# A decode block on one core: V in 64 KB runs and one transfer a head, head 0's keys in the repeated body, wq in 32 KB runs

## The chip, the cores and the metric

The kernel runs on one core of one Trainium2 chip. The metric is the device time of one execution in microseconds (us); lower is better. Inputs lie in HBM, TensorE (PE) multiplies 128x128 tiles out of SBUF into PSUM, VectorE (DVE) and ScalarE (ACT) work on PSUM and SBUF, and SyncE (SP) issues the transfers, which all run on the core's 16 DMA engines. A profile row "PE L566" is an instruction of TensorE recorded at line 566; "PEld" is its weight load.

## The reference

One token passes through a transformer block: layer norm, attention of 32 heads over a cache of 32768 keys and values each, output projection and residual, then a second layer norm and a dense layer with a mish activation.

```python
# B=1, D=512, H=32, Dh=128, Sk=32768, F=1376, all bfloat16
def _A_ref(x, k_cache, v_cache, wq, wo):
    q = (x @ wq).reshape(B, Sq, H, Dh).transpose(0, 2, 1, 3)
    scores = jnp.einsum("bhqd,bhkd->bhqk", q, k_cache) * (Dh ** -0.5)
    p = softmax(scores)
    o = jnp.einsum("bhqk,bhkd->bhqd", p, v_cache)
    return o.transpose(0, 2, 1, 3).reshape(B, Sq, H * Dh) @ wo
def _B_ref(x, w1, b1, w2):
    h = jnp.einsum("bsd,df->bsf", x, w1) + b1
    sp = log1p(exp(-abs(h))) + where(h > 0, h, 0)
    return jnp.einsum("bsf,fd->bsd", h * tanh(sp), w2)
h  = x + _A_ref(layernorm(x), k_cache, v_cache, wq, wo)
h2 = h + _B_ref(layernorm(h), w1, b1, w2)
```

The K and the V of one head are 8 MB each, so 512 MB are read from HBM for one token.

## The kernel before

**Slots.** SBUF holds a ring of six slots of 4 MB (32 KB in each of 128 partitions). Slots 0 and 1 take the two halves of a head's K, slots 2 and 3 those of its V, slot 4 wq and later the small weights of the end, slot 5 wo. Head 0's K is an exception: its halves go into slots 2 and 3 (`HOMES`), so that head 1's K can be fetched without waiting for anything, and head 0's V then waits for head 0's K.

**Transfers.** `order` is the list of all transfers, and SP issues them in that order (`start`, L439): wq, K of head 0, wo, then for each head h its two K halves and the two V halves of head h-1, at the end the rows of wo for the last head, the two V halves of head 31, w1 and w2. Ahead of each it waits until its slot is free (`freed_by`): a K or V half waits for the same half of the head before it. A half takes keys `half*16384` and on, and partition p holds 128 neighbouring keys of that half, one run of 32 KB in HBM. The first V half of head 31 (`SPLITV`) is issued in two pieces and the second (`LASTV`) in four (64, 32, 16 and 16 keys a partition), so that the work at the end can follow the data closely. wq is read as four runs of 8 KB in each partition (`(k p) n -> p k n`), with x laid out to match by a small matmul (L498).

**Work.** For each K half (`keys`, `k_group`) PE transposes 128 tiles (L566), eight to a group, DVE copies each group out of PSUM (L569), and PE forms the scores with the query as moving operand, one column for each tile (L544, three groups behind). The softmax needs the maximum over all 32768 scores (L610 to L623, with two small matmuls), one `exp` on ACT (L626) and a sum (L631). `pv` multiplies the V tiles with the probabilities (L595, 256 matmuls a head), and `oev` divides by the sum (L605).

**Order on the engines.** Head 0's keys and softmax are written out straight. Then `S.rounds(1, H, head, rest, mid)` makes a loop on PE and DVE: round i does `head(i)` (keys and maximum of head i) and `rest(i)` (the sum of head i-1, its `pv` in three parts with the steps `soft_a` and `soft_b` of head i between them, `oev`, and the `exp` of head i). In PE's loop the blocks lie in memory in the order top, head, mid, rest; `mid` (output projection of heads 0 to 30) runs once, in place of `head`, before the `rest` of the last round. The code of the second half of the block, `project_last` and on, follows the loop. `in_final` puts a wait into the loop body that holds only in the last round.

Of the kernel before, what the change touches and what calls it, by code (L numbers as in the profile page):

```python
# [21 lines left out]
class _Sched:  # L22
# [73 lines left out]
    def rounds(self, first, end, head, rest, mid):  # L96


        both = (head, rest)
        self.end = end  # L100
        if not self.emit:
            for n in range(first, end):
# [4 lines left out]
                self._play(tuple(LOOPED), n, (rest,), self.log["rest"])  # L107
            mid()
            self.log[PE][end] = {}
            self._play((PE,), end, (rest,), self.log["rest"])  # L110
            return
        if self.only == PE:
            self._pe_rounds(first, end, head, rest, mid)
            return
        if self.only == DVE:
# [3 lines left out]
            with self.nc.Fori(first, end, engines=OrderedEngineSet([e]), hint_back_edge=True,  # L119
                              head_slot={e: 0}) as i:  # L120
                self.counter = i
                self._play(tuple(LOOPED), first, both)
            self.counter, self.mute = None, True
            for n in range(first + 1, end):
                self._play(tuple(LOOPED), n, both)
            self.mute = False
        else:
            for n in range(first, end):
                self._play(tuple(LOOPED), n, both)
        mid()  # L130
        self._play((PE,), end, (rest,), self.log["rest"])

    def _pe_rounds(self, first, end, head, rest, mid):
# [3 lines left out]
        names = [f"rounds_{x}_{nc.next_id()}" for x in ("top", "head", "mid", "rest", "done")]  # L137
        top, n_head, n_mid, n_rest, done = names
# [4 lines left out]
        self.reg = regs[e]  # L143
        with nc.body(top, valid_engines=on):
            hint = t.mark_branch_hint_location()
            t.br_eq(regs[e], end, on_true=n_mid, on_false=n_head)
        with nc.body(n_head, valid_engines=on):
            self.loop_waited = {}
            self.counter = nc.snap(regs, min_val=first, max_val=end - 1)
            self._play(tuple(LOOPED), first, (head,))  # L150
            nc.br(n_rest, engines=on)
        self.counter = None
        with nc.body(n_mid, valid_engines=on):
            self.uncounted = True
            mid()
            self.uncounted = False
            nc.br(n_rest, engines=on)
        with nc.body(n_rest, valid_engines=on):
            self.loop_waited = {}
            self.counter = nc.snap(regs, min_val=first, max_val=end)  # L160
            self._play(tuple(LOOPED), first, (rest,), self.log["rest"])
# [4 lines left out]
        for n in range(first + 1, end):  # L166
            self._play(tuple(LOOPED), n, (head, rest))
# [5 lines left out]
    def in_final(self, eng, wait):  # L173
        if eng != PE or not self.emit or self.only != PE or self.counter is None:
            return
        with self.engines[PE].If_eq(self.reg, self.end):
            self.engines[PE].wait_ge(self._handle(wait[0]), wait[1])
# [80 lines left out]
def build_kernel(nc, A_x, A_k_cache, A_v_cache, A_wq, A_wo, B_w1, B_b1, B_w2, out):  # L258
    D = A_x.shape[-1]
    Dh = 128  # L260
# [65 lines left out]
    b1r = sb([FJ + 1, 128], BF16, "b1r")  # L326
    lnx = sb([128, 2, 2, 128], F32, "lnx")
# [21 lines left out]

    sem = nc.alloc_semaphore  # L350
    kinds = [PE, ACT, DVE, POOL, SP, "exp", "pmax", "gmax", "qc", "nb", "rcp", "oev", "A", "B", "C", "qkh", "pv", "fv", "ov"]
# [3 lines left out]
    s_x = sem("s_x")  # L355
    s_b1 = sem("s_b1")
# [14 lines left out]
    SPLITV = ("v", H - 1, 0)  # L371
    LASTV = ("v", H - 1, HALVES - 1)
    TAIL = [64, 32, 16, 16]
    piece_sems = [sem(f"piece{i}") for i in range(1, len(TAIL))]

    s_wl = sem("wl")
    s_early = sem("early")
# [5 lines left out]
    AFTER = {WQ: [], WO: [], WL: [WQ]}  # L383
    for half in range(HALVES):
        HOMES["k", 0, half] = HALVES + half
        AFTER["k", 0, half] = AFTER["k", 1, half] = []
        AFTER["v", 0, half] = [("k", 0, half)]

    def slot_of(what):
# [4 lines left out]
        return what[2] + (HALVES if what[0] == "v" else 0)  # L394
# [14 lines left out]
    def freed_by(what):  # L409
        if what[0] in ("w1", "w2"):  # L410
            return []
        if what == SPLITV:
            return [f"early{H - 2}"]
        if what in AFTER:
            return [free_name(x) for x in AFTER[what]]
# [10 lines left out]
    wol_v = w12[:, W2:W2 + D]  # L426

    events = {}

    def program(S):  # L430
# [10 lines left out]
        for what in order:  # L441
# [3 lines left out]
            if what[0] == "wq":  # L445
                start(wq_v, A_wq.rearrange("(k p) n -> p k n", k=KC), ready[slot])
# [13 lines left out]
            else:  # L460
                kind, h, half = what
                cache = A_k_cache if kind == "k" else A_v_cache
                rows = cache[0, h, half * 128 * TPS:(half + 1) * 128 * TPS, :].rearrange("(p r) d -> p (r d)", r=TPS)
                if what == SPLITV:
                    at = TPS // 2 * Dh
                    start(flat[:, 0:at], rows[:, 0:at], s_early)
                    S.wait(SP, [free_name(("v", H - 2, 0))])
                    start(flat[:, at:], rows[:, at:], ready[slot])
                elif what == LASTV:
                    at = 0  # L470
                    for n, s in zip(TAIL, [ready[slot]] + piece_sems):
                        start(flat[:, at * Dh:(at + n) * Dh], rows[:, at * Dh:(at + n) * Dh], s)
                        at += n
                    assert at == TPS
                else:
                    start(flat, rows, ready[slot])
# [5 lines left out]
        S.dma(ACT, lambda: a.dma_start(xr[:, :], A_x[0, 0, :].rearrange("(c m) -> c m", c=KC)).then_inc(s_x, 16))  # L482
        if S.emit and S.only == ACT:
# [16 lines left out]
        S.step(DVE, lambda: v.tensor_copy(lnx[:, 0, 0, 0:128:32], X_REG), name="lnh0", waits=["xT"])  # L500

        def layernorm(n):
# [12 lines left out]
            S.step(ACT, lambda: a.activation(rstd, lnv, ACTF.Exp, scale=-0.5), name=f"lnr{n}", waits=[f"lnln{n}"])  # L515
# [21 lines left out]
        def scores(h, col0, bg):  # L537
            last = col0 + GT == SCOLS
            for r in range(GT):
                names = [f"qkh{h}"] if last and r == GT - 1 else []  # L540
                waits = [f"ev{bg}"] if r == 0 else []
                if r == 0 and col0 == 0:
                    waits += [f"qc{h}"] + ([f"exp{h - 1}"] if h >= 1 else [])
# [32 lines left out]
        def pv(h, half, r0, r1):  # L576
            what = ("v", h, half)
            vt = tiles_of(what)
            for r in range(r0, r1):
                col = half * TPS + r  # L580
                waits = []
                if col == 0:
                    waits.append(f"exp{h}")
                if r == 0:
                    waits.append(ready_wait(what))
                elif half == HALVES - 1 and r in starts:
                    S.in_final(PE, (piece_sems[starts.index(r) - 1], 16))
                names = []
                if half == 0 and r == 0:
                    S.in_final(PE, (s_early, 16))  # L590
                if half == 0 and r == TPS // 2 - 1:
                    names = [f"early{h}"]
                if r == TPS - 1:
                    names = [free_name(what)] + ([f"pv{h}"] if half == HALVES - 1 else [])
                S.step(PE, lambda r=r, col=col: t_.matmul(o_ps[:, 0:1], vt[:, r, :], pbuf[:, col:col + 1],  # L595
                                                          start=(col == 0), stop=(col == SCOLS - 1)),
                       name=(names or None), waits=waits, kind="pv" if half == HALVES - 1 else ("ov" if r < TPS // 2 else "fv"))

        starts = [sum(TAIL[:i]) for i in range(len(TAIL))]

# [85 lines left out]
        S.rounds(1, H, head, rest, mid)  # L686
# [3 lines left out]
        S.step(DVE, lambda: v.tensor_tensor(lnx[:, 1, 0, 0:128:32], yps[:, 0:KC], lnx[:, 0, 0, 0:128:32], ALU.add), name="lnh1", waits=["y"])  # L690
# [75 lines left out]
```

## Time and profile before

| | |
|---|---|
| median of 3 runs | 1282.67 us (1282.5 to 1282.84) |
| profiled execution: its own time | 1282.67 us |
| profiled execution: span, first to last instruction | 1280.9 us |
| bytes read from HBM | 548.21 MB, 428 GB/s over the span |
| busy: PE, PE weight loads, DVE, ACT | 80%, 77%, 56%, 2% |
| chain that ended last, by engine | DMA 82%, PE 13%, DVE 2%, issue 2% |

The span leaves out 1.77 us that lie around the first and the last instruction. The rate is a mean over the span; the rows of the 40 slices tell how it runs in time. The chain follows the last instruction back, at each step to what released it: a share of a transfer in it is time in which the next work waited for that transfer or for the transfers queued ahead of it.

### The profile page before, as it was taken

The page shows a single profiled execution, that of the slowest core. Times are in us where ns is not written, and L with a number is a line of the kernel's source. Part 1 is how long each engine was busy: PE and PEld are TensorE (multiplying, and loading weights), DVE is VectorE, ACT ScalarE, POOL GpSimd, SP SyncE. Part 2 cuts the span into 40 slices and gives each one's busy share as a digit, 9 for nine tenths or more (in the row PEclk, how much of TensorE's full clock was granted, in tenths as well). Part 3 has the DMA queues.
Part 4 walks back from the last instruction along what each step waited for, and adds up shares of the span by engine and source line. Part 5 has one row for each costly group of instructions (what it writes and reads, how often), then busy time and mean ns, then how long its engine had stood idle before and what let it go on. Part 6 is the DMA issues. An engine that isn't in the chain of part 4 may idle for free.

```text
span 1280.9 us, 52609 instructions
## 1 busy us (share of the span) xinstructions
PE 1019.4 (80%) x25125; PEld 990.5 (77%) x25125; DVE 711.4 (56%) x1248; ACT 20.6 (2%) x70; POOL 1.8 (0%) x8
## 2 busy tenths in 40 slices
PE   3869977779877789877798777798777898777886
PEld 3768877779777788777788777797777787777885
DVE  2746664456654456644566544566544566444661
ACT  0000000000000000000000000000000000000000
POOL 0000000000000000000000000000000000000000
PEclk9878876778876788776788776788777788677885
DMA  9999999999999999999999999999999999999998
GB/s 404 428 423 435 432 429 434 432 431 433 430 434 432 430 435 431 431 433 430 434 432 430 433 433 429 433 432 432 432 430 435 431 430 433 433 431 433 430 418 343
DMA packets 21873, 548.47 MB, mean 428 GB/s; under 512 B 2304, under 2 KB 3808, under 8 KB 4576
## 3 DMA queue, kind: packets, MB, share of 16 engines
q1 hardware_dynamic: 21784, 548.22, 99.7%
q8 instruction: 13, 0.21, 0.1%
q14 instruction: 4, 0.03, 0.0%
q0 software_dynamic: 64, 0.00, 0.0%
q10 hardware_dynamic: 8, 0.00, 0.0%
HBM read 548.21 MB, written 0.00 MB: 428 GB/s over the span
## 4 chain that ended last, share of the span: by engine, by line
DMA 82%; PE 13%; DVE 2%; issue 2%; SPq 0%; ACT 0%; DVEq 0%
DMA ring<-in_A_v_cache_dram 81%; PE ops L595 9%; PE tps L566 2%; DVE ering L569 2%; DMA ring<-in_A_k_cache_dram 2%; PE sps L544 1%; SPq L439 0%; PE sps L701 0%; PE hlp L616 0%; PE hlp L621 0%; PE tps L717 0%; PE hlp L631 0%; PE hlp L508 0%; DVE pmax L610 0%; ACT lns L513 0%
## 5 line engine op out<-in xcount | busy, mean ns | idle before, releaser
L566 PE MATMUL tps<-identb,ring 128*128 128x128 bf16 x8192 | 667.2, 232 | 187.9 <-DMA ring<-in_A_k_cache_dram 185.0
L569 DVE COPY ering<-tps 128x1024 bf16<-128x1024 bf16 x1024 | 668.2, 692 | 236.9 <-PE tps L566 230.2
L566 PEld LDWEIGHTS tps<-identb,ring 128*128 128x128 bf16 x8192 | 521.1, 104 | 191.3 <-DMA ring<-in_A_k_cache_dram 187.5
L544 PE MATMUL sps<-qcur,ering 128*128 128x1 bf16 x8192 | 343.2, 164 | 7.7 <-DVE ering L569 6.7
L544 PEld LDWEIGHTS sps<-qcur,ering 128*128 128x128 bf16 x8192 | 308.8, 97 | 10.8 <-DVE ering L569 9.8
L595 PEld LDWEIGHTS ops<-pbuf,ring 128*128 128x128 bf16 x8192 | 223.8, 103 | 57.6 <-DMA ring<-in_A_v_cache_dram 35.9
L595 PE MATMUL ops<-pbuf,ring 128*128 128x1 bf16 x8192 | 232.0, 165 | 40.0 <-DMA ring<-in_A_v_cache_dram 35.1
L605 DVE TENSOR_TENSOR oT<-ops,rtotc 128x1 f32 x31 | 5.0, 161 | 142.2 <-PE ops L595 142.2
L618 DVE TENSOR_REDUCE gmax<-hlp 1x1 f32<-1x128 f32 x32 | 8.9, 278 | 65.6 <-PE hlp L616 65.6
L623 DVE TENSOR_SCALAR nbias<-hlp 128x1 f32<-128x1 f32 x32 | 5.1, 158 | 65.0 <-PE hlp L621 65.0
L626 ACT ACTIVATE pbuf<-sps,nbias 128x256 bf16<-128x256 f32 x32 | 15.2, 474 | 1231.4 <-PE ops L595 1184.9
L610 DVE TENSOR_REDUCE pmax<-sps 128x1 f32<-128x256 f32 x32 | 13.6, 425 | 15.4 <-PE sps L544 15.4
L621 PE MATMUL hlp<-gmax,onesmat 1*128 1x1 f32 x64 | 18.3, 353 | 0.4 <-DVE gmax L618 0.4
L616 PE MATMUL hlp<-ident,pmax 128*1 128x128 f32 x64 | 17.4, 369 | 0.5 <-DVE pmax L610 0.5
L631 PE MATMUL hlp<-esum,onesmat 128*128 128x1 f32 x64 | 12.3, 262 | 6.0 <-issue 5.9
L621 PEld LDWEIGHTS hlp<-gmax,onesmat 1*128 1x128 f32 x64 | 15.6, 300 | 1.1 <-DVE gmax L618 0.7
L631 PEld LDWEIGHTS hlp<-esum,onesmat 128*128 128x128 f32 x64 | 9.9, 195 | 8.3 <-issue 6.0
L523 PE MATMUL hlp<-xnT,ring 128*128 128x1 bf16 x128 | 3.6, 165 | 9.7 <-DMA ring<-in_A_wq_dram 9.7
L523 PEld LDWEIGHTS hlp<-xnT,ring 128*128 128x128 bf16 x128 | 3.5, 104 | 9.8 <-issue 9.8
L633 DVE RECIPROCAL rtotc<-hlp 128x1 f32<-128x1 f32 x32 | 5.1, 159 | 10.1 <-PE hlp L631 10.1
L605 DVE TENSOR_TENSOR oL<-ops,rtotc 128x1 bf16<-128x1 f32 x1 | 0.2, 163 | 12.0 <-PE ops L595 12.0
L527 DVE CAST qT<-hlp 128x32 bf16<-128x32 f32 x1 | 0.2, 191 | 11.9 <-PE hlp L523 11.9
(59 smaller groups left out, 41.4 us busy)
## 6 DMA issues: line engine op xcount, KB each, us to landing
ring<-in_A_k_cache_dram SPq DMA_DIRECT2D x64, 4096.0 KB, 26.8
ring<-in_A_v_cache_dram SPq DMA_DIRECT2D x62, 4096.0 KB, 31.3
ring<-in_A_v_cache_dram SPq DMA_DIRECT2D x3, 2048.0 KB, 11.3
ring<-in_A_wq_dram SPq DMA_DIRECT2D x1, 4096.0 KB, 12.4
ring<-in_A_wo_dram SPq DMA_DIRECT2D x1, 4096.0 KB, 41.6
ring<-in_B_w_dram SPq DMA_DIRECT2D x1, 1376.0 KB, 18.1
ring<-in_B_w_dram SPq DMA_DIRECT2D x2, 640.0 KB, 20.1
ring<-in_A_v_cache_dram SPq DMA_DIRECT2D x1, 1024.0 KB, 13.5
```

Of the source, the lines that this page charges most:

```text
L523: S.step(PE, lambda h=h, kc=kc: t_.matmul(Q_REG[:, h:h + 1], wq_v[:, kc, h * Dh:(h + 1) * Dh], xnT[:, 0, kc:kc + 1], start=(kc == 0), stop ...
L544: S.step(PE, lambda r=r: t_.matmul(S_ps[:, col0 + r:col0 + r + 1], ering[:, bg % NE, r, :], qcur[:, :], start=True, stop=True), name=(name ...
L566: S.step(PE, lambda r=r: t_.matmul(tb[:, r * 128:(r + 1) * 128], kt[:, gi * GT + r, :], identb[:, :], is_transpose=True, start=True, stop= ...
L569: S.step(DVE, lambda: v.tensor_copy(ering[:, bg % NE, :, :].rearrange("p r d -> p (r d)"), tb[:, :]), name=f"ev{bg}", waits=[f"trb{bg}"], ...
L595: S.step(PE, lambda r=r, col=col: t_.matmul(o_ps[:, 0:1], vt[:, r, :], pbuf[:, col:col + 1], start=(col == 0), stop=(col == SCOLS - 1)), n ...
L605: S.step(DVE, lambda: v.tensor_tensor(out_column(), o_ps[:, 0:1], rtotc[:, :], ALU.mult), name=f"oev{h}", waits=[f"pv{h}", f"rcp{h}"], kin ...
L610: S.step(DVE, lambda: v.tensor_reduce(pmax[:, :], S_ps[:, 0:SCOLS], AXX, ALU.max), name=f"pmax{h}", waits=[f"qkh{h}"], kind="pmax")
L616: S.step(PE, lambda: t_.matmul(A_REG, pmax[:, :], ident[:, :], start=True, stop=True), name=f"A{h}", waits=[f"pmax{h}", "ident", f"rcp{h - ...
L618: S.step(DVE, lambda: v.tensor_reduce(gmax[:, :], A_REG, AXX, ALU.max), name=f"gmax{h}", waits=[f"A{h}"], kind="gmax")
L621: S.step(PE, lambda: t_.matmul(B_REG, onesm[0:1, :], gmax[:, :], start=True, stop=True), name=f"B{h}", waits=[f"gmax{h}", "consts0"], kind ...
L626: S.step(ACT, lambda: a.activation(pbuf[:, :], S_ps[:, 0:SCOLS], ACTF.Exp, bias=nb[:, :], scale=SC, accum_out=esum[:, :]), name=f"exp{h}", ...
L631: S.step(PE, lambda: t_.matmul(C_REG, onesm[:, :], esum[:, :], start=True, stop=True), name=f"C{h}", waits=[f"exp{h}"], kind="C")
```

## The change

- V of heads 0 to 29 is one transfer of 8 MB into slots 2 and 3 together. Partition p holds keys 256p to 256p+255, one run of 64 KB in HBM. The V of head 30 is issued in two halves and that of head 31 in the six pieces that it had before, in the new layout (`PARTS`); each piece waits for the step of the head before that has read the same columns (`v_done`).
- K follows the same layout of keys, since scores and V must match: a half is a run of 32 KB out of each 64 KB of HBM.
- Head 0's K goes into slots 0 and 1 as every other, so head 1's K now waits for it, and head 0's V waits for nothing.
- The loop on PE starts with head 0: `head(0)` is its body in round 0, and a new block `turn` (the softmax of head 0) stands ahead of `top` and is entered from the end of `head` in round 0 alone. The straight code for head 0's keys goes. The blocks lie in the order turn, top, mid, head, rest. On the other engines head 0 is written out straight as before.
- wq is read as one run of 32 KB in each partition (`(p k) n -> p (k n)`), and x comes in a second time in the matching layout by a transfer of 8 bytes a partition on ACT's queue (`xc`). The old layout of x, by way of the matmul, is kept for the residual (`xres`).
- The waits of the last rounds (`in_round`) name their round; the body of `rest` has six of them, where it had four.

```diff
-    def _pe_rounds(self, first, end, head, rest, mid):
+    def _pe_rounds(self, end, head, turn, rest, mid):
...
-        nc.regs_mov(regs, first)
-        t.addr_align(256, offset=0, max_nops=0)
+        nc.regs_mov(regs, 0)
         nc.br(top, engines=on)
         self.reg = regs[e]
+        with nc.body(n_turn, valid_engines=on):
+            turn()
+            nc.regs_alu(regs, regs, 1, op=ALU.add)
+            t.addr_align(256, offset=0, max_nops=0)
+            nc.br(top, engines=on)
         with nc.body(top, valid_engines=on):
             hint = t.mark_branch_hint_location()
             t.br_eq(regs[e], end, on_true=n_mid, on_false=n_head)
...
+        with nc.body(n_head, valid_engines=on):
+            self.loop_waited = {}
+            self.counter = nc.snap(regs, min_val=0, max_val=end - 1)
+            self._play(tuple(LOOPED), 0, (head,))
+            t.br_lt(regs[e], 1, on_true=n_turn, on_false=n_rest)
...
+    V_EVENTS = (TPS // 2, TPS)
+    PARTS = {H - 2: [(0, TPS), (TPS, SCOLS)],
+             H - 1: [(0, TPS // 2), (TPS // 2, TPS), (TPS, 192), (192, 224), (224, 240), (240, SCOLS)]}
     order = [WQ] + halves("k", 0) + [WO]
     for h in range(1, H):
-        order += halves("k", h) + halves("v", h - 1)
-    order += [WL] + halves("v", H - 1) + W1P + W2P
+        order += halves("k", h) + [("v", h - 1)]
+    order += [WL, ("v", H - 1)] + W1P + W2P
...
     def freed_by(what):
-        if what[0] in ("w1", "w2"):
+        if what == WL:
+            return [free_name(WQ)]
+        if what[0] not in ("k", "v") or what[1] == 0 or (what[0] == "v" and what[1] in PARTS):
             return []
...
-        return [free_name((what[0], what[1] - 1, what[2]))]
+        return [free_name((what[0], what[1] - 1) + what[2:])]
     def tiles_of(what):
-        return ring[:, slot_of(what), :].rearrange("p (r d) -> p r d", d=Dh)
+        n = 1 if len(what) > 2 else HALVES
+        return ring[:, slot_of(what):slot_of(what) + n, :].rearrange("p s (r d) -> p (s r) d", d=Dh)
+    def keys_of(cache, h):
+        return cache[0, h, :, :].rearrange("(p r) d -> p r d", r=SCOLS)
...
-                start(wq_v, A_wq.rearrange("(k p) n -> p k n", k=KC), ready[slot])
+                start(flat, A_wq.rearrange("(p k) n -> p (k n)", k=KC), ready[slot])
...
-                rows = cache[0, h, half * 128 * TPS:(half + 1) * 128 * TPS, :].rearrange("(p r) d -> p (r d)", r=TPS)
...
+                if what[0] == "k":
+                    start(tiles_of(what), keys_of(A_k_cache, h)[:, what[2] * TPS:(what[2] + 1) * TPS, :], ready[slot])
+                    continue
+                for n, (r0, r1) in enumerate(PARTS.get(h, [(0, SCOLS)])):
+                    if h in PARTS:
+                        S.wait(SP, [v_done(h - 1, r1)])
+                    start(tiles_of(what)[:, r0:r1, :], keys_of(A_v_cache, h)[:, r0:r1, :],
+                          piece_sems[h][n - 1] if n else ready[slot])
...
+        S.dma(ACT, lambda: a.dma_start(xc[:, :], A_x[0, 0, :].rearrange("(p k) -> p k", k=KC)).then_inc(s_xc, 16))
...
-        S.step(DVE, lambda: v.tensor_copy(lnx[:, 0, 0, 0:128:32], X_REG), name="lnh0", waits=["xT"])
+        S.step(DVE, lambda: v.tensor_copy(lnx[:, 0, 0, 0:128:32], xc[:, :]), name="lnh0", waits=["lnz", (s_xc, 16)])
+        S.step(DVE, lambda: v.tensor_copy(xres[:, :], X_REG), name="xres", waits=["xT"])
...
-        keys(0, 0)
-        keys(0, 1)
-        flush(0)
-        soft_max(0)
-        soft_a(0)
-        soft_b(0)
-        soft_exp(0)
+        def turn():
+            soft_a(0)
+            soft_b(0)
+            soft_exp(0)
...
             soft_c(t)
-            pv(t, 0, 0, TPS // 2)
+            pv(t, 0, TPS // 2)
             S.unless_final(PE, "soft_a", lambda: soft_a(i))
-            pv(t, 0, TPS // 2, TPS)
+            pv(t, TPS // 2, TPS)
             S.unless_final(PE, "soft_b", lambda: soft_b(i))
-            pv(t, 1, 0, TPS)
+            pv(t, TPS, SCOLS)
             oev(t)
...
-        S.rounds(1, H, head, rest, mid)
+        S.rounds(H, head, turn, rest, mid)
```

More of the change, by code (lines that the diff above doesn't have):

```diff
@@ L94, in _play, with rounds @@
         self.round, self.looped = None, ()
-    def rounds(self, first, end, head, rest, mid):
-        both = (head, rest)
+    def rounds(self, end, head, turn, rest, mid):
         self.end = end
         if not self.emit:
-            for n in range(first, end):
+            for n in range(end):
                 for e in LOOPED:
@@ L110, in rounds @@
             self._play((PE,), end, (rest,), self.log["rest"])
+            del self.log[DVE][0]
             return
         if self.only == PE:
-            self._pe_rounds(first, end, head, rest, mid)
+            self._pe_rounds(end, head, turn, rest, mid)
             return
+        head(0)
+        turn()
         if self.only == DVE:
@@ L165, in _pe_rounds @@
         self.mute = True
-        for n in range(first + 1, end):
-            self._play(tuple(LOOPED), n, (head, rest))
+        for n in range(1, end):
+            self._play(tuple(LOOPED), n, (head, rest) if n > 1 else (head,))
         mid()
@@ L171, in _pe_rounds, with in_round @@
         nc.switch_bb(done)
-    def in_final(self, eng, wait):
+    def in_round(self, eng, n, wait):
         if eng != PE or not self.emit or self.only != PE or self.counter is None:
             return
-        with self.engines[PE].If_eq(self.reg, self.end):
+        with self.engines[PE].If_eq(self.reg, n):
             self.engines[PE].wait_ge(self._handle(wait[0]), wait[1])
@@ L348, in build_kernel @@
     OX_PS = T_f[2][:, 0:32]
+    V_EVENTS = (TPS // 2, TPS)
     sem = nc.alloc_semaphore
-    kinds = [PE, ACT, DVE, POOL, SP, "exp", "pmax", "gmax", "qc", "nb", "rcp", "oev", "A", "B", "C", "qkh", "pv", "fv", "ov"]
+    kinds = [PE, ACT, DVE, POOL, SP, "exp", "pmax", "gmax", "qc", "nb", "rcp", "oev", "A", "B", "C", "qkh", "pv"] + [f"pv{r}" for r in V_EVENTS]
     kinds += [f"{k}{i}" for k in ("ev", "tr") for i in range(2 * GPS)]
@@ L355, in build_kernel @@
     s_x = sem("s_x")
+    s_xc = sem("s_xc")
     s_b1 = sem("s_b1")
@@ L460, in program @@
             else:
-                kind, h, half = what
-                cache = A_k_cache if kind == "k" else A_v_cache
-                rows = cache[0, h, half * 128 * TPS:(half + 1) * 128 * TPS, :].rearrange("(p r) d -> p (r d)", r=TPS)
[L464 to L476, printed above, removed]
+                h = what[1]
+                if what[0] == "k":
[6 more added lines that the diff above has]
+                          piece_sems[h][n - 1] if n else ready[slot])
         S.dma(SP, lambda: sp.dma_start(out[0, 0, :].rearrange("(c m) -> c m", c=KC), outr[0:128:32, :]).then_inc(s_out, 16),
@@ L573, in k_group, with pv @@
             flush(KEEP)
-        def pv(h, half, r0, r1):
-            what = ("v", h, half)
+        def pv(h, r0, r1):
+            what = ("v", h)
             vt = tiles_of(what)
             for r in range(r0, r1):
-                col = half * TPS + r
                 waits = []
-                if col == 0:
-                    waits.append(f"exp{h}")
                 if r == 0:
[L585 to L599, printed above, removed]
+                    waits += [f"exp{h}", ready_wait(what)]
+                for n in PARTS:
+                    for i, (first, _) in enumerate(PARTS[n][1:]):
+                        if r == first:
+                            S.in_round(PE, n + 1, (piece_sems[n][i], 16))
+                names, kind = [], "pv"
+                if r + 1 in V_EVENTS:
+                    names, kind = [f"pv{h}_{r + 1}"], f"pv{r + 1}"
+                if r == SCOLS - 1:
+                    names, kind = [free_name(what), f"pv{h}"], "pv"
+                S.step(PE, lambda r=r: t_.matmul(o_ps[:, 0:1], vt[:, r, :], pbuf[:, r:r + 1],
+                                                 start=(r == 0), stop=(r == SCOLS - 1)),
+                       name=(names or None), waits=waits, kind=kind)
         def oev(h):
@@ L689, in program @@
         project_last()
-        S.step(DVE, lambda: v.tensor_tensor(lnx[:, 1, 0, 0:128:32], yps[:, 0:KC], lnx[:, 0, 0, 0:128:32], ALU.add), name="lnh1", waits=["y"])
+        S.step(DVE, lambda: v.tensor_tensor(lnx[:, 1, 0, 0:128:32], yps[:, 0:KC], xres[:, :], ALU.add), name="lnh1", waits=["y", "xres"])
         layernorm(1)
```

58 lines of the change are left out of this document (24 added, 34 removed).

## The prediction, made before the result was known

> **What bounds the kernel now.** I read the page first: the busy shares, the 40 slices, the chain by engine, the queues.
>
> ```profile
> PE 1019.4 (80%) x25125; PEld 990.5 (77%) x25125; DVE 711.4 (56%) x1248; ACT 20.6 (2%) x70; POOL 1.8 (0%) x8
> GB/s 404 428 423 435 432 429 434 432 431 433 430 434 432 430 435 431 431 433 430 434 432 430 433 433 429 433 432 432 432 430 435 431 430 433 433 431 433 430 418 343
> q1 hardware_dynamic: 21784, 548.22, 99.7%
> q8 instruction: 13, 0.21, 0.1%
> ...
> DMA 82%; PE 13%; DVE 2%; issue 2%; SPq 0%; ACT 0%; DVEq 0%
> ```
>
> No compute engine is full, the data queue q1 keeps the 16 DMA engines busy for 99.7% of the span, and the chain is transfers. The slices say where it isn't even: 404 to 428 in the first three, 429 to 435 until the tail. So three questions carry the forecast: the rate in the rounds, what is lost ahead of them, and whether the queue still never runs dry. The chain in order of time gives the round, and the windows the rate.
>
> ```profile
> 161.95 3.59 PE ops L595 x128
> ...
> 1249.92 3.59 PE ops L595 x128
> ```
>
> Both rows are the second `pv` half starting as its V lands, of heads 2 and 30: 28 rounds in 1087.97 us, 38.856 a round, 9.714 for each half of 4 MB. Next, PE and SP inside one round.
>
> ```profile
> 667.05 3.57 PE L595 MATMUL ops<-pbuf,ring 128*128 128x1 bf16 x128 [1.04 <-DMA ring<-in_A_v_cache_dram]
> 676.76 3.32 PE L566 MATMUL tps<-identb,ring 128*128 128x128 bf16 x32 [6.14 <-DMA ring<-in_A_k_cache_dram]
> 698.22 0.33 SPq L439 DMA_DIRECT2D ring<-in_A_k_cache_dram  x1
> 699.32 0.37 PE L631 MATMUL hlp<-esum,onesmat 128*128 128x1 f32 x2
> 703.80 0.58 PE L621 MATMUL hlp<-gmax,onesmat 1*128 1x1 f32 x2
> 705.90 3.57 PE L595 MATMUL ops<-pbuf,ring 128*128 128x1 bf16 x128 [1.52 <-DMA ring<-in_A_v_cache_dram]
> ```
>
> PE waits twice: 6.14 us for K and 1.52 for the second V half. `head` takes 676.76 to 699.32, 22.6 us; `rest` without its wait takes 699.32 to 704.38 and another 3.57, so 8.6. That is 31.2 of 38.86. The jump from `head` over `mid` to `rest` shows no gap ahead of L631.
>
> The start, where the slices are low:
>
> ```profile
> 0.75 0.46 SPq L439 DMA_DIRECT2D ring<-in_A_wq_dram  x1
> 2.41 0.17 DVE L500 COPY lnx<-hlp 128x4 f32<-128x4 f32 x1 [0.31 <-PE hlp L498]
> 4.67 0.29 DVE L516 TENSOR_SCALAR xnT<-lnx,lns 128x4 bf16<-128x4 f32 x1 [0.60 <-ACT lns L515]
> 13.32 3.55 PE L523 MATMUL hlp<-xnT,ring 128*128 128x1 bf16 x128 [9.70 <-DMA ring<-in_A_wq_dram]
> 24.44 3.50 PE L566 MATMUL tps<-identb,ring 128*128 128x128 bf16 x32 [7.58 <-DMA ring<-in_A_k_cache_dram]
> 36.05 12.44 SPq L439 DMA_DIRECT2D ring<-in_A_v_cache_dram  x2
> 41.76 0.45 PE L566 MATMUL tps<-identb,ring 128*128 128x128 bf16 x5 [0.85 <-issue]
> 47.68 0.45 PE L566 MATMUL tps<-identb,ring 128*128 128x128 bf16 x5 [0.57 <-issue]
> 54.05 3.59 PE L566 MATMUL tps<-identb,ring 128*128 128x128 bf16 x32 [3.14 <-DMA ring<-in_A_k_cache_dram]
> 85.80 0.58 PE L631 MATMUL hlp<-esum,onesmat 128*128 128x1 f32 x2 [5.90 <-issue]
> ```
>
> wq lands at 13.32, K of head 0 at 24.44, K of head 1 at 54.05. Against 9.714 a half: 13.32 to 24.44 is 11.12 for one, 1.41 too long; 24.44 to 54.05 is 29.61 for three (K, wo, K), 0.47 too long; 54.05 to 161.95 is 107.90 for eleven, 1.05 too long. The stream loses **2.93 us** between the first landing and the even rounds, though SP has transfers queued the whole time. In the same stretch PE stands still for its own code ("issue"): 0.85 and 0.57 us inside head 0's keys, 5.90 at the first jump to `rest`. Between the stalls at 41.76 and 47.68 lie eight groups of eight transposes and eight scores, each a load and a matmul: 256 instructions for one stall. The queue "instruction" moved 13 packets of 0.21 MB together, 16 KB each, so 256 instructions a packet. They run on the same 16 engines (0.1% of 16 x 1280.9 us over 13 is 1.6 us each, between 0.8 and 2.4 by the rounding), and a packet sits on one engine, while a data transfer lands when its slowest engine is done. What an engine loses stays lost, since none is ever idle. My reading: the slowest engine was hit twice, at 1.41 to 1.47 us a hit.
>
> **The change part by part.** The sum is made against the profiled execution, 1282.67 us (1.77 around the span), equal to the median.
>
> *V in 64 KB runs.* What a packet costs beside its bytes comes from the rate at two packet sizes: wq in 8 KB runs, K and V in 32 KB runs (windows; the last two columns are the DMA share and GB/s).
>
> ```profile
> 4.00:12.00 8.00, 0.00 (x0) 0.00 (x0) 0.36 (x2) 0.50 (x2) 0.00 (x0) 1.00 1.01 424
> 200.00:588.50 388.50, 314.88 (x7740) 306.69 (x7740) 220.89 (x380) 5.66 (x20) 0.00 (x0) 0.76 1.00 432
> ```
>
> At 424 GB/s one of 16 engines spends 309.1 ns on 8 KB, at 432 it spends 1213.6 on 32 KB; (4 x 309.1 - 1213.6) / 3 = 7.6 ns a packet (6.7 to 8.6 by the rounding). V of a head is 16 data packets and two completions on each engine, then 8 and one: 9 x 7.6 = 68 ns a head, 30 heads **-2.05 us**. No row has a 64 KB packet; if the gap is in the bytes and not in the packet, the gain is 0, and 2.3 is the most. I take 2.05, since both rows are loads by the same queue. A round would be 38.79.
>
> *V whole: nothing.* `rest` can start its `pv` only when all 8 MB have landed, where half of it was done ahead. Then 8.6 us follow the landing, and the next K lands 9.71 after it: PE is ready 1.1 us early, and its idle time moves from 6.14 ahead of K to in front of V. Two more tests in `rest` are free as the four now there are: 128 matmuls around three of them run in 3.57 us, 28 ns each. The next V is issued 8.6 us after the landing instead of 5.0; K covers the queue for 19.43. From issue to flowing data it takes at most 2.9 us (wq is issued at 0.75, lands 12.57 later, and 9.71 of that are bytes), so 7.9 are left. If that cover were gone, every us would cost thirty.
>
> *Head 0 in the loop.* 256 columns x (transpose, score) x (load, matmul) = 1024 instructions leave the program, four packets of 13. `mid`, `head` and `rest` keep their size, and the loop's code stayed loaded before: from 200 to 1200 us the only "issue" wait of more than 0.1 us a round is this one at `soft_a`.
>
> ```profile
> PEld ops L595 <- issue: 9.6, 25, 0.4
> ```
>
> 9 packets remain, 8 of them before the rounds are even (the last one, as I take it, is for the code of the end, before and after). If engines take them in turn, at most two hits out of 12 means 6 to 11 engines in the turn; with 8 or more, 8 packets hit no engine twice. So **-1.47 us**; the ends are 0 (still two hits) and -2.93. K of head 1 now waits for head 0's. Its first half is issued near 36, when the queue holds work until wo lands at 24.44 + 2 x 9.71 = 43.9; its second near 48.5, when K lands at 54.05 and data must follow, so 5.6 less 2.9, 2.7 us, are spare. The first pass meets code as cold as before: the jump over `mid` to `head` may stall 5.9 us, but PE idles 7.58 ahead of 24.44. I take 0, with 2 us as the other end. V of head 0 queues behind that second K on SP, and has 9.7 us. `turn` runs after the last K tile is freed; a 5.9 us stall there delays `head(1)`, whose first K slot is wanted only when V of head 0 is through, 54.05 + 3 x 9.71 = 83.2.
>
> *wq and xc.* 32 data packets an engine become 8, -0.18 us; xc adds 8 tiny ones and a completion, +0.07: **-0.11**. `lnh0` now waits for xc, and all of DVE's layer norm behind it, then PE's 128 matmuls. From 2.41 to 4.96 that chain is 2.55 us, so xc may land at 10.7 and q still waits for wq; and q itself ends 7.58 us before K is there. The load of b1's ten short rows, issued beside wq's, took 5.3 us:
>
> ```profile
> b1r<-in_B_b_dram POOLq DMA_DIRECT2D x1, 2.5 KB, 5.3
> ```
>
> so 0, and 0 at the other end too unless xc takes 18 us. By the Trainium skill, DMA: Bandwidth & Descriptors, section "Queues, rings and completion order", an engine takes turns between queues packet by packet; by that, eight rows of xc could each wait out a 32 KB packet and land near 12 us as an estimate, which the 7.58 us still hide. No run here shows it.
>
> *The end: nothing.* V30 in halves and V31 in six pieces keep the waits of before (PE's progress in V29 and V30), and `mid`, now ahead of `head`, ends in a jump like the one that cost nothing.
>
> ```profile
> 1254.87 15.06 DMA ring<-in_A_v_cache_dram
> 1269.93 0.27 issue
> ```
>
> The last piece lands at 1269.93, and 11 us of small steps follow, all unchanged.
>
> Sum: -2.05 - 1.47 - 0.11 = -3.63, **1279.0 us**; with every term at its better end 1277.3, with none 1282.7.
>
> **The rivals.** *The read pattern (slower).* K is now a 32 KB run out of each 64 KB, and the engines' runs of K and V start twice as far apart. If HBM serves that worse, each 0.2% of rate costs 2.5 us of the 1243 that K and V stream (128 halves). The decisive point is 0.3%: from there it eats the gain of 3.6. For it: the new spacing stands in no row. Against it: 424 for wq and 432 for K and V come from different spacings, and their gap is small. If K and V fell to wq's rate, 1.9%, it would be 23.5 on top of the forecast: **1302.5 us**. The Trainium skill, same page, section "Latency and other measured facts", says that copies slow when the rows of the partitions lie a large power of two apart, from 214 GB/s to 207 at 512 KiB and to half at 4 MiB; at this kernel's 64 KiB its list shows nothing, so by it the loss would be small, and 3% as an estimate were it there already. No row of before bears on it.
>
> *Code packets hit one engine twice still.* Then -2.16: **1280.5**. The 2.93 may have been something else, though it comes in steps and only while code loads.
>
> *The packet cost is not per packet* (or long runs are cut in two on their way): then -1.58: **1281.1**. The change would then not do what its name says.
>
> *The queue runs dry once,* at head 1's second K: cold code in the first pass takes longer than the 2.7 us spare. Two us beyond give **1281.0**.
>
> *The whole V starves every round (slower):* the 7.9 us of cover are less than I think. One us a round is +30: 1309.
>
> **How the numbers follow.** Forecast 0.55, read pattern 0.14, two hits 0.10, no packet cost 0.10, dry once 0.07, starved rounds 0.04. A measurement of this kernel can tell 0.2%, 2.57 us, from no change: 1280.1 to 1285.2. Only the forecast lies below it, 0.55; the three middle cases give 0.27, the two that lose 0.18. The forecast alone reaches from 1277.8 to 1280.1. The range goes up through the middle cases to 1285.0 and leaves the two that lose out, 0.18, and below 1277.6 some 0.02.
>
> **What would show it.** Right: V's issues x30 at 8192 KB, q1 at some 17,080 packets (30 x 144 + 384 fewer); rounds of 38.79; 9 instruction packets; 1.5 us lost ahead of the even rounds; PE idle some 1 us ahead of K and 5 ahead of V. Wrong: rounds of 38.86 or more, a slice under 428 between the third and the tail, 2.9 us lost still, or idle DMA engines between 50 and 55 us.

## The result, and the profile after

The changed kernel takes 1285.55 us (median of 17 runs, 1283.9 to 1287.29), the kernel before 1282.77 (17 runs, 1282.48 to 1282.93): 1.0023 of its time, 95% interval 1.0015 to 1.003 (ratios here are of the means of the runs). It is slower by about 2.8 us, where 3.6 us less were predicted. The kernel before repeats within 0.5 us and the changed one spreads over 3.4: something in it depends on chance. Its profiled execution is the slowest of the 17, 1287.29 us with a span of 1285.5.

From the page of the changed kernel: the slices' rate, the queues of data, of code and of ACT, the chain by engine.

```profile
GB/s 405 344 432 431 440 426 447 416 436 430 447 430 425 427 435 430 437 436 435 422 433 436 443 426 425 431 434 438 428 438 424 430 434 440 438 424 426 433 409 335
q1 hardware_dynamic: 17080, 548.22, 99.2%
q8 instruction: 9, 0.15, 0.0%
q10 hardware_dynamic: 152, 0.00, 0.0%
DMA 77%; PE 22%; issue 1%; DVE 0%; SPq 0%; ACT 0%
```

Packets (17,080) and code packets (9) are as forecast, and one slice stands out: the second, from 32 to 64 us, moves 344 GB/s where before moved 428. At 428 the missing share of that slice is (428 - 344) / 428 x 32.1 = 6.3 us. The even rounds, by V of head 2 and, 28 rounds on, the second half of V of head 30 in the chain (start, length):

```profile
137.80 30.50 DMA ring<-in_A_v_cache_dram
...
1223.88 30.61 DMA ring<-in_A_v_cache_dram
```

(1223.88 - 137.80) / 28 = 38.789 us a round, where 38.856 was measured before and 38.79 forecast. So the rounds gain what they should. But V of head 2 lands at 137.80 + 30.50 = 168.30, where before had it at 161.95: 6.35 us are lost ahead of the rounds. The timeline of the start shows the place (start, length, what; in brackets the idle time before, and what ended it):

```profile
1.34 0.36 ACTq L489 DMA_DIRECT2D xc<-in_A_x_dram  x1
15.64 0.17 DVE L507 CAST lnx<-xc 128x4 f32<-128x4 bf16 x1 [13.54 <-DMA xc<-in_A_x_dram]
18.25 3.58 PE L532 MATMUL hlp<-xnT,ring 128*128 128x1 bf16 x128 [1.40 <-DVE xnT L525]
33.47 3.59 PE L575 MATMUL tps<-identb,ring 128*128 128x128 bf16 x32 [11.65 <-issue]
45.70 10.68 SPq L452 DMA_DIRECT2D ring<-in_A_k_cache_dram  x2
56.42 0.43 SPq L452 DMA_DIRECT2D ring<-in_A_v_cache_dram  x1
```

x arrives 14.3 us after its issue, so q starts at 18.25 and not at 13.32. Then PE stands 11.65 us for its own code ("issue"), and head 0's keys start at 33.47 instead of 24.44. "Issue" names only a wait without a releaser in the profile. That it is code fits the code queue, of which two packets start in this wait (DMA view of 21.8 to 33.5 us), and e3 below, where head 0 does not jump and the wait is gone.

```profile
q8 instruction: 2, 0.03, 1.1%
```

K of head 1 waits for head 0's keys: SP can issue its first half only at 45.70 and its second near 56. Windows of the same kernel (PE clock, DMA share and GB/s are the last three columns; a packet counts where it starts, so a 32 KB packet still flows for some 1.2 us into an empty row, and a share can pass 1):

```profile
41.00:42.00 1.00, 1.00 (x31) 1.00 (x29) 1.00 (x3) 0.00 (x0) 0.00 (x0) 1.00 0.23 82
43.00:44.00 1.00, 1.00 (x31) 1.00 (x29) 1.00 (x3) 0.00 (x0) 0.00 (x0) 1.00 0.00 0
45.00:46.00 1.00, 1.00 (x31) 1.00 (x28) 1.00 (x3) 0.00 (x0) 0.00 (x0) 1.00 0.00 0
46.00:47.00 1.00, 1.00 (x30) 1.00 (x28) 1.00 (x2) 0.00 (x0) 0.00 (x0) 1.00 1.57 442
```

From 43 us on no packet starts until the issue at 45.70: the queue has run dry. It is the first half of K that comes too late here. Over the whole stretch the engines are busy 0.83 of the time at 340 GB/s, where before had 1.01 and 430 (after, then before):

```profile
35.00:64.00 29.00, 26.16 (x536) 25.30 (x533) 21.44 (x36) 0.57 (x2) 0.00 (x0) 0.94 0.83 340
35.00:64.00 29.00, 23.11 (x494) 21.79 (x492) 19.85 (x35) 0.56 (x2) 0.00 (x0) 0.88 1.01 430
```

### The profile page after: what moved, and what is told of

It is laid out like the page before. It is cut to its first block, busy times and chain, and to the rows that moved or that the text cites. A ratio compares the mean times of both kernels' runs of the same rounds, so it can differ in the third digit from the quotient of the medians.

```text
span 1285.5 us, 52593 instructions
## 1 busy us (share of the span) xinstructions
PE 1020.4 (79%) x25125; PEld 995.5 (77%) x25125; DVE 712.0 (55%) x1249; ACT 20.6 (2%) x70; POOL 1.8 (0%) x8
## 3 DMA queue, kind: packets, MB, share of 16 engines
q1 hardware_dynamic: 17080, 548.22, 99.2%
## 4 chain that ended last, share of the span: by engine, by line
DMA 77%; PE 22%; issue 1%; DVE 0%; SPq 0%; ACT 0%
DMA ring<-in_A_v_cache_dram 75%; PE ops L601 17%; DMA ring<-in_A_k_cache_dram 2%; PE tps L575 1%; PE hlp L620 1%; PE hlp L625 1%; PE sps L553 0%; SPq L452 0%; PE sps L702 0%; PE tps L718 0%; PE hlp L516 0%; ACT lns L521 0%; DVE xnT L525 0%; DVE outr L723 0%; PE yps L676 0%
## 5 line engine op out<-in xcount | busy, mean ns | idle before, releaser
L601 PEld LDWEIGHTS ops<-pbuf,ring 128*128 128x128 bf16 x8192 | 226.4, 104 | 190.5 <-DMA ring<-in_A_v_cache_dram 168.8
L625 PEld LDWEIGHTS hlp<-gmax,onesmat 1*128 1x128 f32 x64 | 15.6, 300 | 1.1 <-DVE gmax L622 0.7
## 6 DMA issues: line engine op xcount, KB each, us to landing
ring<-in_A_wq_dram SPq DMA_DIRECT2D x1, 4096.0 KB, 12.4
```

Source lines behind the costliest of these rows:

```text
L601: S.step(PE, lambda r=r: t_.matmul(o_ps[:, 0:1], vt[:, r, :], pbuf[:, r:r + 1], start=(r == 0), stop=(r == SCOLS - 1)), name=(names or Non ...
L625: S.step(PE, lambda: t_.matmul(B_REG, onesm[0:1, :], gmax[:, :], start=True, stop=True), name=f"B{h}", waits=[f"gmax{h}", "consts0"], kind ...
```

## The experiments

The theory: the gains are real, and the queue runs dry at the start because head 0 comes late. The rival theories: wq's and K's new runs are read more slowly by themselves; or the loop's code is what costs, whatever SP has queued. "V0 ahead" below means that the first half of V of head 0 is put ahead of K of head 1 in `order`; "V1 in halves" that V of head 1 comes as two transfers, so that each can be issued when its half is free. Medians in us, with the range of the runs; the kernel before took 1282.84 to 1282.88 beside them.

| run | x for q | head 0 | V0 ahead | V1 in halves | median | range |
|---|---|---|---|---|---|---|
| changed | late | loop | no | no | 1285.55 | 1283.9 to 1287.29 |
| e1 | as before, wq in 8 KB runs | loop | no | no | 1282.83 | 1280.65 to 1285.65 |
| e2 | early (SP) | loop | no | no | 1283.03 | 1280.74 to 1285.55 |
| e3 | late | straight | no | no | 1284.4 | 1281.35 to 1285.04 |
| e4 | late | loop | yes | no | 1283.45 | 1281.57 to 1285.26 |
| e5 | late | loop | yes | yes | 1281.26 | 1279.22 to 1283.38 |
| e6 | early (SP) | loop | yes | yes | 1279.49 | 1279.36 to 1279.69 |
| e7 | early (ACT) | loop | yes | yes | 1279.18 | 1278.88 to 1279.3 |
| e8 | as before, wq in 8 KB runs | loop | yes | yes | 1279.2 | 1279.07 to 1279.31 |
| e9 | early (ACT) | loop | yes | no | 1280.69 | 1280.35 to 1282.17 |
| e10 | early (ACT) | loop | no | yes | 1283.02 | 1280.83 to 1287.04 |
| e11 | as before, wq in 8 KB runs | straight | no | yes | 1280.58 | 1280.43 to 1282.25 |

**e1: wq and x as before.**

```diff
-start(flat, A_wq.rearrange("(p k) n -> p (k n)", k=KC), ready[slot])
+start(wq_v, A_wq.rearrange("(k p) n -> p k n", k=KC), ready[slot])
```
(and `lnh0` from the matmul again, without `xc`)

> Undoes the wq and x part alone: wq again in 8 KB runs, the layer norm again on the x that comes by way of the matmul, no 8-byte rows. Theory A (the queue runs dry because head 0 starts late, half of that through xc): q ends near 17 instead of 21.8, head 0 starts at 28 to 29 instead of 33.5, K of head 1 is issued near 41 and 51 instead of 45.7 and 56.1, almost nothing is left of the dry stretch: 1279.5 to 1281. Rival B (xc is hidden; only the jump into the loop's cold code is late, and it ends at 33 whatever q does): 1285.5 as the changed kernel. Rival C (the loss is in the rounds or at the end): 1285.5 too, with head 0 early.

Measured: 1282.83, ratio 0.9996 (0.9987 to 1.0005). 2.7 us come back, but not all. From its timeline:

```profile
13.34 3.55 PE L531 MATMUL hlp<-xnT,ring 128*128 128x1 bf16 x128 [9.65 <-DMA ring<-in_A_wq_dram]
27.51 3.46 PE L574 MATMUL tps<-identb,ring 128*128 128x128 bf16 x32 [10.62 <-issue]
38.78 16.48 SPq L452 DMA_DIRECT2D ring<-in_A_k_cache_dram  x2
47.99 0.69 PE L574 MATMUL tps<-identb,ring 128*128 128x128 bf16 x5 [1.98 <-issue]
```

Windows of the same kernel:

```profile
50.00:52.00 2.00, 2.00 (x34) 2.00 (x33) 1.25 (x3) 0.00 (x0) 0.00 (x0) 0.50 0.84 352
52.00:54.00 2.00, 2.00 (x33) 2.00 (x31) 1.30 (x2) 0.00 (x0) 0.00 (x0) 0.50 0.00 0
```

q is on time again, and head 0 still starts 3 us late, behind 10.62 us of waiting for code: the jump into the loop is a cause of its own. Then a second code stall of 1.98 us comes inside the keys; behind it the granted clock is 0.50, the second K half is issued only at 38.78 + 16.48 = 55.3, and no packet starts from 52 to 54.

**e2: x first on SP's queue.**

```diff
+start(xc[:, :], A_x[0, 0, :].rearrange("(p k) -> p k", k=KC), s_xc)
```
(ahead of wq, and no longer on ACT's queue)

> Keeps wq in 32 KB runs and issues the 8-byte rows of x on SP's queue ahead of wq instead of on ACT's beside it. Theory A: the rows go out before any 32 KB packet and land by 4 us, layer norm is done by 7, q waits for wq as before; 1279.3 to 1281, as with wq undone. Rival B: 1285.5. A variant of A in which the 8-byte rows are slow by themselves, without 32 KB packets between them: xc lands late still and the time stays at 1285.

Measured: 1283.03, ratio 1.0004 (0.9995 to 1.0013). The same 8-byte rows, now ahead of wq in one queue (DMA issues of the page: KB, us to landing):

```profile
xc<-in_A_x_dram SPq DMA_DIRECT2D x1, 1.0 KB, 1.8
```

1.8 us instead of 14.3, with the long wq runs kept, and the time is that of e1. So what wq's part of the change costs is x's place in the queues, not wq's pattern. Its profiled execution was one of the quick ones (1281.54): it issued the second K half at 51.5 and moved 419 GB/s from 35 to 64 us.

**e3: head 0 straight on PE**, the rest as changed.

```diff
+        head(0)
+        turn()
         if self.only == PE:
             self._pe_rounds(end, head, turn, rest, mid)
             return
-        head(0)
-        turn()
```
(and `nc.regs_mov(regs, 1)`, without the block `turn`)

> Undoes the other part alone: head 0's keys stand again as straight code ahead of PE's loop (blocks top, head, mid, rest); xc, the slots and V in 64 KB runs stay as changed. Theory A: no jump, so head 0 starts 0 to 6 us after q, at 22 to 28 instead of 33.5, and the queue runs dry little or not at all; 13 instruction packets again, so the slowest engine is hit twice: 1280.5 to 1282.5. If the two hits cost nothing: 1279 to 1281. Rival B' (the wait of K of head 1 for head 0's K is too late however head 0 is coded): over 1284.

Measured: 1284.4, ratio 1.0006 (0.9997 to 1.0015), above what the theory expected and where the rival B' had put it. The trace decides between them. Head 0 starts at 22.97, behind the late q without a code stall. On its page the second slice is full (436), and the fourth is not (364):

```profile
GB/s 403 436 417 364 447 425 425 433 432 431 436 429 452 411 441 426 452 431 417 432 431 451 427 425 425 440 427 442 425 440 426 431 434 431 448 431 422 428 427 352
```

Its timeline in the fourth slice:

```profile
90.74 0.58 PE L631 MATMUL hlp<-esum,onesmat 128*128 128x1 f32 x2 [5.90 <-issue]
96.75 0.46 PE L597 MATMUL ops<-pbuf,ring 128*128 128x1 bf16 x12 [1.74 <-issue]
103.67 0.88 PE L597 MATMUL ops<-pbuf,ring 128*128 128x1 bf16 x18 [2.92 <-issue]
104.58 0.33 SPq L448 DMA_DIRECT2D ring<-in_A_v_cache_dram  x1
```

Windows of the same kernel:

```profile
102.00:104.00 2.00, 0.25 (x3) 0.17 (x4) 0.00 (x0) 0.00 (x0) 0.00 (x0) 0.50 0.00 0
```

A second dry place, which the prediction did not have: V of head 1 is now one transfer and waits for all of head 0's `pv`, and that is the first pass through `rest`, with three code stalls (5.90, 1.74, 2.92 us) at half the clock. Before had nearly the same stalls, but there the first half of V could be issued at 92.18, behind the first half of `pv`. In the changed kernel's own profiled execution this second place costs nothing (DMA share 1.01 from 96 to 128 us), since the late K of head 1 has put off all that comes behind it.

**e4: V0 ahead**, the rest as changed (x late).

```diff
+    PARTS = {0: [(0, TPS), (TPS, SCOLS)],
...
+    order += [("v", 0)]
     for h in range(1, H):
-        order += halves("k", h) + [("v", h - 1)]
+        order += halves("k", h) + [("v", h - 1) if h > 1 else ("v0b",)]
```

> Takes away the dry queue and leaves head 0 as late as it is: the first half of head 0's V, which waits for nothing, is issued ahead of K of head 1, the second half in its old place. Theory A: head 0 still starts near 33.5, but 9.7 us more are queued, so K of head 1 is in time; no dry stretch: 1278.8 to 1280. Rival C (the loss is elsewhere): 1285.

Measured: 1283.45, ratio 1.0007 (0.9998 to 1.0016), where 1280 at most was expected. On its page the second slice is full again (430) although head 0 starts at 33.24: a full queue hides a late head 0. The fourth is short (384), as in e3:

```profile
GB/s 402 430 426 384 428 456 426 409 442 426 458 426 426 426 429 439 442 426 426 437 431 442 426 426 440 428 436 432 432 448 413 439 429 444 436 430 424 428 428 352
```

Its timeline there:

```profile
101.97 0.89 PE L605 MATMUL ops<-pbuf,ring 128*128 128x1 bf16 x20 [2.67 <-issue]
102.89 0.33 SPq L454 DMA_DIRECT2D ring<-in_A_v_cache_dram  x1
```

Windows of the same kernel:

```profile
102.00:103.00 1.00, 0.80 (x20) 0.63 (x19) 0.00 (x0) 0.04 (x1) 0.00 (x0) 0.50 0.00 0
```

**e5: V0 ahead and V1 in halves** (x late).

```diff
-    PARTS = {H - 2: [(0, TPS), (TPS, SCOLS)],
+    PARTS = {0: [(0, TPS), (TPS, SCOLS)],
+             1: [(0, TPS), (TPS, SCOLS)],
+             H - 2: [(0, TPS), (TPS, SCOLS)],
```
(and the lines of e4)

> e4 and one thing more: V of head 1 in two halves, the first issued when half of head 0's V is used up; xc stays late. Theory A2 (after e1 to e4: there are two places where the queue runs dry in the first round, K of head 1, which waits for head 0's keys, and V of head 1, which waits for all of head 0's V in code that is loaded for the first time; e4 covered the first and met the second at 100 to 118 us): no dry stretch is left although head 0 starts at 33 us; eight hits of code packets on eight engines leave the slowest some 2.1 us behind instead of 3.4; 1282.9 - 2.05 - 1.3 - 0.1 = 1279.4, and the spread of the runs shrinks under 2 us. Rival D (runs differ by something other than the dry stretch, for instance by the granted clock): 1282 to 1284, spread of 4 us still.

Measured: 1281.26, ratio 0.9987 (0.9978 to 0.9996), faster than before. Its best run, 1279.22, is at the forecast, but the runs still spread over 4 us. The profiled execution (1280.02) shows no dry stretch (DMA share 1.01 from 35 to 64 and from 90 to 125 us), so a dry queue does not explain why it is slower than e7 below; it does show a 2.01 us code stall with the clock at 0.50 behind it, and its K halves 14.2 us apart. What the longer runs look like was not seen.

**e6, e7: x early as well**, ahead of wq on SP, or first on ACT's queue (`xc` ahead of `xr`).

> e5 with xc issued ahead of wq on SP's queue as in e2, which costs 0.4 us at the very start. Theory A2: lateness of head 0 is harmless once transfers are queued, so nothing is gained beside e5 and the 0.4 us show: 1279.8. If the late xc matters by itself: 1 us or more below e5.

> e5 with xc issued first on ACT's queue, beside wq at 0.74 us, and the other x behind it. If the 8-byte rows come ahead of the first 32 KB packets, xc lands near 3 us and the time is that of e5, 1279.4; if they are dealt out between the packets, the other x follows late too and xc lands near 14 us: same time by theory A2, 1279.4, since nothing waits for head 0.

Measured: 1279.49, ratio 0.9973 (0.9963 to 0.9984), and 1279.18, ratio 0.9971 (0.996 to 0.9982), with a range of 0.3 to 0.4 us. e7 beats both kernels. The theory expected nothing from an early x once the queue is covered, and it brings 1.8 to 2.1 us in the median and takes the spread away; why is not shown. First on ACT's queue, issued at 0.74 us beside wq at 0.75, x takes 6.2 us. e7's start in its timeline:

```profile
13.17 3.55 PE L537 MATMUL hlp<-xnT,ring 128*128 128x1 bf16 x128 [2.50 <-DMA ring<-in_A_wq_dram]
27.07 3.59 PE L580 MATMUL tps<-identb,ring 128*128 128x128 bf16 x32 [10.35 <-issue]
39.28 12.95 SPq L455 DMA_DIRECT2D ring<-in_A_k_cache_dram  x2
```

Its slices:

```profile
GB/s 407 426 428 434 433 439 441 424 423 434 441 435 437 419 430 435 442 433 435 420 431 434 441 439 425 424 433 440 433 437 420 431 433 446 431 435 421 430 427 347
```

The stall for code is as long as ever (10.35 us) and head 0 as late as in e1, yet no slice between the first and the last is short: the transfers do not wait for it.

**e8: as e7, with wq and x as before.**

> e5 with wq in 8 KB runs and no xc, as in e1. By the packet cost of 7.6 ns wq costs 0.18 us more and xc's 0.07 are saved: 1279.5. If wq in long runs is worth more than that, it shows here: over 1280.

Measured: 1279.2, ratio 0.9971 (0.996 to 0.9982): the same as e7. wq in 32 KB runs, with the second load of x that it needs, is worth nothing that can be measured.

**e9, e10: e7 without V1 in halves, and without V0 ahead.**

> q early and the first half of V of head 0 ahead of K of head 1, but V of head 1 whole. If V of head 1 lacks cover by itself: the first two passes of cold code in `rest` delay its issue to about 97 us, 4 us later than with its halves (93.0), and the time lies near 1281, spread over more than 1 us. If an early q alone gives it enough cover: 1279.2 and a spread of 0.4, as with both.

> q early and V of head 1 in halves, but K of head 1 ahead of V of head 0 as in the changed kernel. If K of head 1 is the thin place even with q early (head 0 starts 27 instead of 24.4, so the second K is issued near 52 to 56): near 1281 with a spread of 3 us. If the early q is enough: 1279.2.

Measured: e9 1280.69, ratio 0.9985 (0.9976 to 0.9994); e10 1283.02, ratio 1.0004 (0.9994 to 1.0013), range 6.2 us. Each cover is needed, even with q on time. In e9 the thin stretch lies where the theory puts it, ahead of V of head 1's late issue (timeline):

```profile
100.63 0.33 SPq L454 DMA_DIRECT2D ring<-in_A_v_cache_dram  x1
```

Windows of the same kernel:

```profile
99.00:100.00 1.00, 0.24 (x4) 0.15 (x3) 0.00 (x0) 0.00 (x0) 0.00 (x0) 0.50 0.38 164
100.00:101.00 1.00, 0.65 (x17) 0.58 (x18) 0.16 (x1) 0.30 (x1) 0.00 (x0) 0.50 0.46 197
```

The issue came at 100.63 where about 97 was expected. From 90 to 125 us e9 moves 408 GB/s, e7 431. e10's profiled execution was its quickest run and shows only a hint of it (419 GB/s from 35 to 64 us, e7 431), so that its long runs go dry at K of head 1 is inferred from the edit, not seen.

**e11: V's runs alone** (wq, x and head 0's code as before, K's layout and slots as changed, V1 in halves).

> V's runs alone: wq, x and head 0 as before, V of head 1 in halves to keep the queue fed. By the prediction's terms -2.05 and nothing else, 1280.8: 12 or 13 code packets as before, rounds of 38.79. If the code packets are worth nothing and V's runs all of the 3.6 us: 1279.2. If the code packets are most of it: near 1282.

Measured: 1280.58, ratio 0.9985 (0.9976 to 0.9994), 2.26 us under the before of its rounds, with 13 code packets. The prediction's term was 2.05.

## Why the prediction was wrong

**V in 64 KB runs: right.** Rounds of 38.789 against 38.79, and 2.26 us by itself in e11 against 2.05. So "no packet cost" falls. The read pattern falls too: the windows of the even stretch give 434 GB/s, more than the 432 of before.

```profile
200.00:588.50 388.50, 314.93 (x7750) 307.63 (x7748) 221.00 (x381) 5.65 (x20) 0.00 (x0) 0.76 1.00 434
```

**Head 0 in the loop, four code packets fewer: right in size.** e8 and e11 differ by that and by V0 ahead, and by 1280.58 - 1279.2 = 1.38 us, where 1.47 was forecast. V0 ahead had nothing to save in e11, whose engines are full without it (DMA share 1.03 from 35 to 64 us, 1.01 from 90 to 125). By the landings of e8, wq's in the timeline, and V's of head 2 in the chain (start, length):

```profile
13.31 3.55 PE L536 MATMUL hlp<-xnT,ring 128*128 128x1 bf16 x128 [9.50 <-DMA ring<-in_A_wq_dram]
```

```profile
131.65 28.85 DMA ring<-in_A_v_cache_dram
```

V of head 2 lands at 160.50, 147.19 us after wq. In between lie nine K and wo transfers of 9.714 and three V of 38.789 - 2 x 9.714 = 19.36, together 145.51. So 1.68 us are lost where before lost 2.93: 1.25 gained by this count. By the same count e11, with before's 13 code packets, loses 2.81 (wq lands at 13.48, V of head 2 at 161.80). That it is the slowest DMA engine being hit once instead of twice was not tested apart.

**wq: -0.11, too small to be seen** (e7 and e8 are equal).

**xc: "so 0", wrong.** The step was the cover: xc could land at 10.7, and then 7.58 us of q's slack were left. xc landed at 15.6. The Trainium skill, DMA: Bandwidth & Descriptors, section "Queues, rings and completion order", has an engine take turns between queues packet by packet; the trace agrees in kind: eight turns of 1.21 us a 32 KB packet are 9.7, with up to 2.9 us from issue to flowing data 12.6 of the 14.3 measured. The estimate from the page, a landing near 12, was closer than the nearest row, b1's 5.3, and still 3.6 us short. By that the step ought still to have held, since q ended at 21.83 with 2.6 us left to 24.44. It failed because the same 7.58 us were also given to the next item.

**The jump over `mid`: "may stall 5.9 us, but PE idles 7.58", wrong twice.** The stall was 10.4 to 11.7 us in every kernel with head 0 in the loop, and it starts only when q is done, so it adds to a late q. Alone it makes head 0 start at 27 and not 24.44 (e7), with xc late at 33.5.

**K of head 1: "2.7 us are spare, I take 0", wrong; this step decides.** Its limit for the second half was right: 48.5 + 2.7 = 51.2. e2 issued it at 51.5 and moved 419 GB/s from 35 to 64 us, where before moved 430; e1 issued it at 55.3 and moved 360, the changed kernel near 56 and moved 340. In the changed kernel the first half failed too: it was forecast near 36, the queue held work until 43.9, and it was issued at 45.70. The 2.7 us spare were used up by the jump alone, which makes head 0 2.6 us late (e7). The rival "the queue runs dry once" was this mechanism; its size, 2 us beyond the forecast, was too small, and it had 0.07.

**V whole: nothing, right in the even rounds and wrong in the first.** The cover of 7.9 us held for 28 rounds. In round 1 `rest` runs code that is loaded for the first time, and V of head 1 waits for all of it (e3, e4 and e9). The prediction looked for the cost of cold code ahead of `head(1)` and not inside the first `pv`.

Taken from e7 one at a time, the covers are worth 2.08 us (x early, e5), 3.84 (V0 ahead, e10) and 1.51 (V1 in halves, e9). All three are missing from the changed kernel, which is 6.37 us above e7; they overlap, as the sum is 7.43. With the covers the prediction's own sum holds: 1279.0 forecast, 1279.18 measured. So the gain of 3.6 us was there and was lost ahead of the rounds. Open are e5's spread, why a q on time ends it, and the last part of the loss in the profiled execution: V of head 2 lands 7.8 us later than in e8, and the second slice explains 6.3 of them against before's rate.

## What to carry to other kernels

A slack can be spent once: list every delay that an edit puts behind the same cover (here the late x and the code stall, both on q's 7.58 us) and add them before calling any of them hidden. Where the data queue is the bound, the first passes of a loop want a deeper queue than the even ones, because code that ran for the first time was late here by up to 11.7 us; a transfer that waits for nothing can be put ahead of those that wait, and in e7 that cost nothing that shows. Here a transfer of many tiny rows was best placed ahead of the large ones, not beside them.

## What the runs showed of the hardware

- The same 1 KB in 8-byte rows took 14.3 us beside a queue of 32 KB packets, 6.2 us when issued first on its own queue, and 1.8 us ahead of wq in the same queue.
- The first jump into the loop cost PE 10.4 to 11.7 us of waiting for code while the data queue was full, the first jump over `mid` 5.9 (e3). Running straight into new code cost 0.2 to 3.2 us at a time.
- A stall of 2 us can be enough to lose the clock. Behind the stall of 1.98 us in e1 the granted clock is 0.50 from 48 to 54 us, and the K half takes 16.5 us, where before it took 12.4; behind stalls of 0.9 to 1.1 us in e7 it stays at 1.00. The Trainium skill, TensorE: Matmul & The Clock Gate, "Part 1: The HAM clock gate", speaks of an idle window of about 3.4 us; here less idle time did it. Whether a stall crosses that point from run to run would explain the spread of the variants with thin cover, but no two executions of one kernel were compared for it.
